# Pooling v of batch 0 and adding the halves of w_theta on VectorE and GpSimd instead of TensorE, in a hand-ordered attention and mixing kernel

## The chip, the core and the metric

The kernel runs on one core of a Trainium2 chip. A core has five engines with a queue of instructions each: TensorE (PE in the profile, its weight loads PEld), VectorE (DVE), ScalarE (ACT), GpSimd (POOL) and SyncE (SP, which here issues the DMAs). An engine takes its instructions strictly in the order in which the program put them, and they wait for each other through semaphores. SBUF is the working memory of 128 partitions. PSUM holds what TensorE writes; DVE and ACT can read it, and in this kernel GpSimd never does.

The metric is the device time of the program in microseconds (us).

## The reference

Pooled attention over 8 batches, 8 heads, 576 positions and 64 channels a head, followed by a mixing block of width 512. All of it is float32 except the weight matrices, which arrive as float64 words:

```python
k_p = k.reshape(B, H, Sp, pool, D).mean(axis=3)      # pool = 8, Sp = 72
v_p = v.reshape(B, H, Sp, pool, D).mean(axis=3)
attn = softmax(q @ k_p^T / sqrt(D));  x = attn @ v_p  # x: B, 576, 512
theta = x @ w_theta
zr, zi = x * cos(theta), x * sin(theta)
y = w_tok_r @ zr + w_tok_i @ zi                       # over the 576 positions
u = x + y
out = u + max(u @ w_ch, 0)
```

## The kernel before

Every batch passes through the same pieces, and each piece is a Python generator that issues a few instructions and yields. Their names are those of the schedule:

- `k`, `v`: the loads of k and v of a batch (0 and 1 are the two main halves, 2 the remainder of 8 pooled rows a head). `K`, `V`: the pooling over 8 neighbours; `K0`, `V0` without a number behind the dot place the pooled tiles for the matmuls (transposed keys in `kpT`, a block-diagonal `Ve` and `Vr` for the values).
- `Q`: loads of q and their transposes. `S`: scores of one tile of 128 positions (`s`), maximum (`mx`), exponential (`e_eps`, `spare`), reciprocal (`ri`), normalised weights (`en`), and for batches 0 and 1 their transposes (`pe`, `per`) on TensorE. `X`: attention output `xT` by `pv`.
- `h0` to `h3`: the four 128-row pieces of w_theta. `w`, `W`: pieces of the token weights w_tok_r and w_tok_i and their transposes `wt` into `WTh`, `WTl`. `c`: w_ch.
- `T`: theta of one tile (`pt`), sine and cosine, products into `z`, with transposes `px`. `Z`: the split of z into a high and a low half (`zh`, `zl`). `M`: mixing over positions (`py`, 27 matmuls each). `F`: the last product (`pf`, 12 matmuls each) and the store.

A float64 weight is taken apart in `to_f32`: two 32-bit words become a leading part `t` and a rest `s`, whose sum is the weight in float32. It is then split into a high part and a low part in TensorE's faster float32 format (`th`, `tl` for w_theta), so that three products stand for one in float32.

Nothing schedules the program: `SCHEDULE` is a list of some 1,900 words written out beforehand, each word advances one piece by one step, and the letter behind it (v, g or a) says which engine takes a step that could go to several. So the order of the words is the order of every queue, SP's included, and the letters spread the elementwise work over DVE, POOL and ACT.

In the kernel before, the flag `V_ON_PE = 1` makes batch 0's values be pooled on TensorE: `pool_on_pe` (L509) multiplies each of the eight neighbours by the identity and lets PSUM add them up, in tile `vpp`. From there DVE copies into `Ve` (L590) and writes `Vr` (L595). K_ON_PE does the same for k of batch 0 and is left alone. The pieces of w_theta are added on TensorE too: `channel_weights` multiplies `t` and `s` by the identity into one PSUM tile `ths` (L351, L352), from which `th` is written with a scale (L355 or L357) and `tl` as the difference (L359).

Batch 0 has a long start of its own: all weights have to be taken apart, split and transposed before its first `py`, while softmax and theta of batch 0 run. Then come seven more batches that overlap with one another.

Of the kernel before, what the change touches and what calls it, by code (L numbers as in the profile page):

```python
# [15 lines left out]
ALU = mybir.AluOpType  # L16
# [26 lines left out]
w4.0 w4.0 W2a W2 T0.1 T0.4a T0.4g T0.3 T0.2 T0.2 T0.2a Q1.2a W2 T0.2 T0.2 T0.2 W2v W2 T0.3 T0.3 v1.1 V1.1g w4.0a
T0.4 w4.0a w4.0 T0.3 T0.3 w3.0v w4.0 Q1.4 W3 T0.4 T0.4 T0.4 T0.4 Q1.4 T0.3a c0 c0 K1 T0.3 T0.3 T0.3 W3a W3 T0.4
# [85 lines left out]
F7.3.1 F7.3.1 F7.3.1 F7.3.0 F7.3.0 F7.3.0 F7.3.1  # L130
"""

EARLY, EXACT, V_ON_PE, K_ON_PE, Q_ON_PE, SUMS_ON_ACT = 2, 1, 1, 1, 2, 2


@with_exitstack
def tile_attn_moe(  # L140
    ctx: ExitStack,
    tc: tile.TileContext,
# [986 lines left out]
```

## Time and profile before

| what | us |
|---|---|
| three runs: median (lowest to highest) | 628.44 (627.2 to 629.33) |
| the profiled execution: its own time | 629.07 |
| its span, first to last instruction | 627.3 |
| 1 core, granted TensorE clock | 0.996 of full |

The profile is one execution, recorded instruction by instruction. Its page gives busy time by engine; other views of the same trace group the instructions by line and shape, follow back the chain of waits that ended last, list a stretch in order of time, or sum the busy time of each engine over chosen stretches. A busy engine is not by itself one that holds up the end: PE's matmuls are pipelined and their ends modelled, so that the busy times of neighbours overlap. Kernel lines are written L517 and so on. Behind the edited function the lines of the changed kernel have numbers lower by two, so that L443 before is L441 after.

### The profile page before, as it was taken

How to read it: one execution, taken by the hardware profiler on the slowest of the kernel's cores; microseconds unless marked ns; L12 is line 12 of the kernel's file. 1: busy time of each engine (PE TensorE's matmuls, PEld its weight loads, DVE VectorE, ACT ScalarE, POOL GpSimd, SP SyncE). 2: the span in 40 equal slices, each digit the busy share in tenths (PEclk: the TensorE clock that was granted, in tenths of full speed). 3: DMA queues.
4: the chain of work that ended last, by engine and by line, in shares of the span. 5: the costliest groups of instructions: out<-in, count | busy, mean ns of one | idle time of the engine just before them, and what ended most of it. 6: DMA issues, size and time to landing. Idle time of an engine off the chain costs nothing.

```text
span 627.3 us, 11459 instructions
## 1 busy us (share of the span) xinstructions
PE 591.2 (94%) x4120; PEld 545.7 (87%) x4120; DVE 481.5 (77%) x878; ACT 312.6 (50%) x674; POOL 350.2 (56%) x380
## 2 busy tenths in 40 slices
PE   4889979999899999899999999999999999999995
PEld 4766769988799879899899989989998999998995
DVE  5599988988897889878967898877886689456433
ACT  4769857688742556247534553237314451345000
POOL 5346545756484656565574667667675375611430
PEclk9999999999999999999999999999999999999999
DMA  9946212475465556554726356443362340511015
GB/s 295 266 135 190 67 43 77 81 124 118 91 125 99 98 100 125 100 95 82 129 58 108 63 107 120 75 85 56 52 100 51 68 65 5 79 20 30 9 20 77
DMA packets 235129, 57.85 MB, mean 92 GB/s; under 512 B 223168, under 2 KB 223680, under 8 KB 235072
## 3 DMA queue, kind: packets, MB, share of 16 engines
q1 hardware_dynamic: 233888, 56.97, 45.2%
q8 instruction: 33, 0.54, 0.4%
q10 hardware_dynamic: 1184, 0.15, 0.2%
q14 instruction: 24, 0.20, 0.1%
HBM read 37.81 MB, written 9.44 MB: 75 GB/s over the span
## 4 chain that ended last, share of the span: by engine, by line
PE 59%; DVE 14%; SPq 10%; DMA 7%; ACT 4%; issue 3%; POOL 3%; DVEq 0%; POOLq 0%; ACTq 0%
PE py L954 24%; PE pf L983 12%; PE pt L888 11%; SPq L814 8%; PE pv L861 4%; PE s L670 3%; DMA out_dram<-R 2%; PE px L898 2%; DMA eraw<-G 1%; DMA WTh_st<-in_moe_w_theta_dram 1%; SPq L1008 1%; DVE kpst L443 1%; DVE R L1002 1%; DMA kpst<-in_k_dram 1%; DVE xT L960 1%
## 5 line engine op out<-in xcount | busy, mean ns | idle before, releaser
L954 PE MATMUL py<-WTh,zh 128*128 128x256 f32 (+1 forms) x576 | 86.5, 297 | 4.4 <-DVE xT L960 2.8
L954 PE MATMUL py<-WTl,zh 128*128 128x256 f32 (+1 forms) x576 | 87.3, 296 | 0.0
L954 PE MATMUL py<-WTh,zl 128*128 128x256 f32 (+1 forms) x576 | 86.0, 294 | 1.0 <-DVE xT L960 1.0
L954 PEld LDWEIGHTS py<-WTh,zh 128*128 128x128 f32 x576 | 80.1, 189 | 5.3 <-DVE xT L960 3.0
L954 PEld LDWEIGHTS py<-WTl,zh 128*128 128x128 f32 x576 | 80.4, 190 | 0.0
L954 PEld LDWEIGHTS py<-WTh,zl 128*128 128x128 f32 x576 | 78.0, 188 | 1.6 <-DVE xT L960 1.2
L940 POOL TENSOR_TENSOR zl<-z,zh 128x640 fp32r<-128x640 f32 (+1 forms) x40 | 59.5, 1509 | 29.4 <-ACT zh L175 28.9
L967 POOL TENSOR_TENSOR ul<-xT,uh 128x320 fp32r<-128x320 f32 (+1 forms) x41 | 34.6, 849 | 43.6 <-DVE uh L177 29.1
L960 DVE TENSOR_TENSOR xT<-py,xT 128x256 f32<-128x256 f32 (+1 forms) x64 | 28.4, 445 | 35.1 <-PE py L954 35.0
L892 ACT ACTIVATE g<-pt,c_magic 128x512 f32<-128x512 f32 x38 | 26.1, 686 | 44.6 <-PE pt L888 36.2
L983 PE MATMUL pf<-uh,chh 128*128 128x256 f32 (+1 forms) x256 | 47.1, 305 | 0.3 <-DVE xT L960 0.3
L888 PE MATMUL pt<-th,xh 128*128 128x512 f32 x160 | 45.3, 405 | 1.4 <-DVE g L894 0.8
L983 PE MATMUL pf<-ul,chh 128*128 128x256 f32 (+1 forms) x256 | 44.8, 296 | 0.0
L983 PE MATMUL pf<-uh,chl 128*128 128x256 f32 (+1 forms) x256 | 44.5, 296 | 0.0
L894 DVE SCALAR_TENSOR_TENSOR g<-g,pt 128x512 f32<-128x512 f32 x38 | 25.8, 680 | 24.1 <-ACT g L892 23.8
L175 ACT CAST uh<-xT 128x320 fp32r<-128x320 f32 (+1 forms) x28 | 12.0, 434 | 63.2 <-DVE xT L960 63.1
L888 PE MATMUL pt<-th,xl 128*128 128x512 f32 x160 | 43.3, 393 | 0.0
L725 ACT ACTIVATE e_eps<-e_eps 128x576 f32<-128x576 f32 (+1 forms) x30 | 20.6, 686 | 45.4 <-DVE e_eps L721 45.3
L888 PE MATMUL pt<-tl,xh 128*128 128x512 f32 x160 | 43.1, 391 | 0.0
L865 ACT ACTIVATE xT<-pv 128x320 f32<-128x320 f32 (+1 forms) x41 | 16.8, 410 | 51.3 <-PE pv L861 45.6
L881 POOL TENSOR_TENSOR xl<-xT,xh 128x512 fp32r<-128x512 f32 x22 | 30.0, 1368 | 20.2 <-ACT xh L175 16.6
L989 DVE SCALAR_TENSOR_TENSOR oT<-pf,xT 128x256 f32<-128x256 f32 (+1 forms) x64 | 28.5, 449 | 14.2 <-PE pf L983 13.5
(252 smaller groups left out, 1491.6 us busy)
## 6 DMA issues: line engine op xcount, KB each, us to landing
out_dram<-R SPq DMA_DIRECT2D x112, 72.0 KB, 2.1
kpst<-in_k_dram SPq DMA_DIRECT2D x15, 512.0 KB, 3.9
vpst<-in_v_dram SPq DMA_DIRECT2D x28, 256.0 KB, 3.9
qsst<-in_q_dram SPq DMA_DIRECT2D x96, 72.0 KB, 2.4
eraw<-G SPq DMA_DIRECT2D x96, 60.0 KB, 2.2
eraw<-G SPq DMA_DIRECT2D x96, 40.0 KB, 2.1
WTh_st<-in_moe_w_theta_dram SPq DMA_DIRECT2D x4, 512.0 KB, 8.6
wcraw<-in_moe_w_ch_dram SPq DMA_DIRECT2D x4, 512.0 KB, 3.3
```

Source lines behind the costliest of these rows:

```text
L814: nc.sync.dma_start(blocks(Ex, jj, i), blocks(Gx, i, jj))
L861: nc.tensor.matmul(pv[:, :gn], l, r, start=i == 0, stop=i == len(terms) - 1)
L881: ENG[pick()].tensor_tensor(xl, xT[:, :, o], f32(xh), ALU.subtract)
L888: nc.tensor.matmul(pt, l[:, c, :], r[:, c, :], start=i == 0, stop=i == 11)
L892: nc.scalar.activation(g, pt, AF.Identity, bias=c_magic)
L894: nc.vector.scalar_tensor_tensor(g, g, MAGIC, pt, ALU.subtract, ALU.subtract)
L940: ENG[pick()].tensor_tensor(zl[:, r], z[:, r, o], f32(zh[:, r]), ALU.subtract)
L954: nc.tensor.matmul(py[:, :n], l[:, kk, :], r[:, kk, t], start=i == 0, stop=i == 3 * NK - 1)
L960: nc.vector.tensor_tensor(u, py[:, :n], u, ALU.add)
L967: ENG[pick()].tensor_tensor(ul[:, c, t], u, f32(uh[:, c, t]), ALU.subtract)
L983: nc.tensor.matmul(pv[:, :n], l[:, kk, o], uhl[r][:, kk, t], start=i == 0, stop=i == 11)
L989: nc.vector.scalar_tensor_tensor(oT, pv[:, :n], 0.0, xT[:, c, t], ALU.max, ALU.add)
```

## The change

Three edits. First, `V_ON_PE` becomes 0, so that `pool` takes its other branch for v of batch 0: three additions in SBUF for each of the three loads (`pool_sum`, L439, halving 512 to 64 columns), each on the engine that the schedule names. `Ve` and `Vr` then read the pooled tile in SBUF, so that their engine is free to be GpSimd too. Second, in `channel_weights` the two matmuls into PSUM are replaced by one elementwise addition of `s` to `t` in SBUF, on DVE or GpSimd, and the scale and the difference that followed read `t` in SBUF in place of the PSUM tile. Third, the whole `SCHEDULE` is replaced, for all eight batches.

```diff
 SCHEDULE = """
-k0.0 w0.0 k0.1 K0.0 K0.1 w0.0 w0.0a w0.0g w0.0 h0 h0 h0g h0a h0 h0 h0v h1 k0.2 h1 h1a h1a h1 h1 h1g Q0.0 K0.0a
...
+D w0.0 w0.0 w0.0v w0.0a h0 h0 h0a w0.0 h0a h0 h0 k0.0 K0.0 h0g h0v K0.0v h1 h1 h1v h0v h0 h1a h1 h1 k0.1 K0.1
...
-EARLY, EXACT, V_ON_PE, K_ON_PE, Q_ON_PE, SUMS_ON_ACT = 2, 1, 1, 1, 2, 2
+EARLY, EXACT, V_ON_PE, K_ON_PE, Q_ON_PE, SUMS_ON_ACT = 2, 1, 0, 1, 2, 2
...
-    def channel_weights(c, w, held_of, scale, raw_of, tmp_of, bank_of):
+    def channel_weights(c, w, held_of, scale, raw_of, tmp_of):
...
-        if bank_of is None:
+        if scale is None:
...
         hi, lo = held_of()
-        sum_ = bank([P, DM], *bank_of(c))
-        nc.tensor.matmul(sum_, ident, t, start=True, stop=False)
-        nc.tensor.matmul(sum_, identr, s, start=False, stop=True)
+        ENG[pick()].tensor_tensor(t, t, f32(s), ALU.add)
         yield
         if pick() == "a":
-            nc.scalar.activation(hi[:, c, :], sum_, AF.Copy, scale=scale)
-        else:
-            nc.vector.tensor_scalar(hi[:, c, :], sum_, scale, None, ALU.mult)
+            nc.scalar.activation(hi[:, c, :], t, AF.Copy, scale=scale)
+        else:
+            ENG[pick()].tensor_scalar(hi[:, c, :], t, scale, None, ALU.mult)
         yield
         nc.vector.scalar_tensor_tensor(
-            lo[:, c, :], sum_, scale, f32(hi[:, c, :]), ALU.mult, ALU.subtract
+            lo[:, c, :], t, scale, f32(hi[:, c, :]), ALU.mult, ALU.subtract
         )
```

What the new order does to the queues is seen at three places.

SP, the first DMAs of the program, before (raw words of w_tok_r are `wraw`, of w_theta `WTh_st`; `kpst`, `early` and `kprst` are the three loads of k):

```order
L461 DMA kpst_0_106<-in_k_dram 128x2x512
L380 DMA wraw_0_108<-in_moe_w_tok_r_dram 128x1152
L461 DMA early<-in_k_dram 128x2x512
L329 DMA WTh_st<-in_moe_w_theta_dram 128x1024 x2
L473 DMA kprst_144<-in_k_dram 64x512
L571 DMA qsst_0_153<-in_q_dram 128x8x64
```

and after:

```order
L378 DMA wraw_0_119<-in_moe_w_tok_r_dram 128x1152
L329 DMA WTh_st<-in_moe_w_theta_dram 128x1024
L459 DMA kpst_0_135<-in_k_dram 128x2x512
L329 DMA WTh_st<-in_moe_w_theta_dram 128x1024
L459 DMA early<-in_k_dram 128x2x512
L471 DMA kprst_168<-in_k_dram 64x512
L569 DMA qsst_0_189<-in_q_dram 128x8x64 x2
```

The same seven loads come first, but the weights are now in front of k, and the second load of q has moved up behind the first.

PE, from the scores of tile 2 to those of tile 4 of batch 0, before:

```order
L670 MATMUL s_2_265<-kpT,qT_152 128x144 x4
L517 MATMUL vpp_304<-early,ident 128x128 x8
L578 MATMUL pq_4_316<-ident,qst_314 128x64 x4
L760 MATMUL pe_0_324<-ident,en_0_272 128x128 x4
L670 MATMUL s_3_0_330<-kpT,qT_152 128x144 x2
L760 MATMUL pe_1_336<-ident,spare 128x128 x4
L517 MATMUL vpp_304<-early,ident 128x128 x8
L519 MATMUL vpp_304<-vprst_369,ident 64x64 x8
L662 MATMUL s_4_383<-kpT,qT_152 64x72 x8
```

and after:

```order
L668 MATMUL s_2_292<-kpT,qT_188 128x144 x4
L758 MATMUL pe_1_318<-ident,spare 128x128 x4
L758 MATMUL pe_0_331<-ident,en_0_261 128x128 x4
L766 MATMUL per_0_337<-ident,en_0_261 64x128
L668 MATMUL s_3_0_349<-kpT,qT_188 128x144 x2
L766 MATMUL per_1_360<-ident,spare 64x128
L660 MATMUL s_4_378<-kpT,qT_188 64x72 x8
```

The three poolings of v are gone between the scores; the 12 warm-up products (`warm`), which stood between the scores of tile 0 and tile 1, are now the first rows of PE.

DVE, in the same stretch, from the maximum of tile 1 on, after:

```order
L702 TENSOR_REDUCE mx_1_232<-s_1_1_227 128x4
L177 COPY qT_188<-pq_2_236 128x4x128
L441 TENSOR_TENSOR early<-early 128x2x256
L441 TENSOR_TENSOR early<-early 128x2x128
L727 RECIPROCAL ri_0_259<-sm_0_248 128x8
L730 TENSOR_TENSOR en_0_261<-e_eps,ri_0_259 128x512
L177 COPY qT_188<-pq_3_263 128x4x128
L355 TENSOR_SCALAR th<-WTh_st 128x512
L357 SCALAR_TENSOR_TENSOR tl<-WTh_st,th 128x512
L177 COPY qT_188<-pq_4_285 128x4x64
L702 TENSOR_REDUCE mx_2_298<-s_2_292 128x8
```

and before:

```order
L704 TENSOR_REDUCE mx_1_231<-s_1_1_226 128x4
L313 TENSOR_SCALAR chh_st<-wsrc_a 128x576
L729 RECIPROCAL ri_0_249<-sm_0_238 128x8
L177 COPY qT_152<-pq_2_252 128x4x128
L177 COPY qT_152<-pq_3_259 128x4x128
L704 TENSOR_REDUCE mx_2_270<-s_2_265 128x8
```

Between the same two maxima DVE now also has two sums of v, a normalisation that GpSimd did before, and `th` and `tl` of a piece of w_theta.

More of the change, by code (lines that the diff above doesn't have):

```diff
@@ new lines @@
+T3.2 T3.2 S4.2 T3.3g T3.3g T3.3 T3.3 T3.4g F2.2.0 T3.4v T3.3 T3.3 E4.0a E4.0g E4.0g E4.0g F2.2.1 F2.2.1 T3.3
+F2.2.0 F2.2.1 K5 S4.3g S4.3g T3.3a T3.4 T3.3 T3.3 T3.3 S4.4 T3.4 T3.4 T3.4 T3.4 Q5.1 Q5.1 T3.4 T3.4 F2.3.1
+F2.3.1 V4g F2.3.0 F2.3.0 X4.0.0 X4.0.0v K5a K5 K5a S5.0 S4.3 Z3.0g X4.0.1 Z3.0g X4.0.1a Z3.1a Z3.1v M3.0.0
+M3.0.0 M3.0.0g S4.4 S4.4 S4.4v S4.4g S5.0 X4.0.2 X4.0.2a M3.0.1 M3.0.1 S4.4 X4.0.3 X4.0.3a T4.0v Q6.0 M3.0.0v
+T4.0g M3.0.1a M3.0.1g S5.0 S5.0 S5.0v v5.1 V5.1g M3.1.1 M3.1.1 M3.1.1a E4.2 S5.1 S5.0v S5.1 S5.1 M3.1.0 S5.1
@@ L1054, in tile_attn_moe @@
                 ),
-                lambda c: ("mm", f"ths{c}", 2),
             ),
```

194 lines of the change are left out of this document (94 added, 100 removed).

## The prediction

> **What bounds the kernel now.** First the page, for the span and the busy shares, then the busy time of each engine by stage (columns: stretch, its length, busy us of PE, PEld, DVE, ACT, POOL, each with its count, then clock, DMA share, GB/s). The stages follow events of the trace: 18.60 is where the first scores of batch 0 start, 34.90 the scores of tile 4, 53.50 the first theta, 91.10 the end of the weights' preparation.
>
> ```profile
> span 627.3 us, 11459 instructions
> PE 591.2 (94%) x4120; PEld 545.7 (87%) x4120; DVE 481.5 (77%) x878; ACT 312.6 (50%) x674; POOL 350.2 (56%) x380
> 5.60:18.60 13.00, 9.43 (x56) 7.24 (x55) 5.22 (x9) 6.68 (x14) 6.36 (x4) 0.87 1.12 309
> 18.60:34.90 16.30, 14.71 (x134) 13.93 (x135) 11.51 (x23) 12.42 (x68) 6.45 (x7) 1.00 0.78 219
> 34.90:41.00 6.10, 4.45 (x35) 2.57 (x31) 5.82 (x15) 4.34 (x16) 3.96 (x6) 1.00 0.15 28
> 41.00:53.50 12.50, 12.34 (x61) 7.31 (x62) 11.66 (x21) 10.40 (x31) 6.06 (x8) 1.00 0.76 238
> 53.50:70.00 16.50, 16.20 (x93) 12.54 (x91) 16.26 (x25) 14.85 (x24) 8.83 (x7) 1.00 0.68 181
> 70.00:91.10 21.10, 15.73 (x107) 13.09 (x106) 19.01 (x31) 16.27 (x30) 12.10 (x10) 1.00 0.09 33
> 95.10:124.00 28.90, 28.20 (x215) 27.65 (x215) 25.49 (x50) 21.09 (x80) 18.42 (x21) 1.00 0.34 85
> 124.00:627.30 503.30, 484.93 (x3406) 456.31 (x3404) 378.51 (x693) 223.92 (x414) 283.62 (x308) 1.00 0.44 79
> ```
>
> The page alone says TensorE, 94%. By stage it is two kernels. From 95.1 on PE is busy 28.20 of 28.90 and 484.93 of 503.30. Before that PE shares the bound with VectorE: from 34.9 to 91.1 DVE is busy 5.82 + 11.66 + 16.26 + 19.01 = 52.75 of 56.2 us. Only from 5.6 to 34.9 has DVE room: 29.3 less 16.73, so 12.6 us. Everything that the change takes from PE stands before 46 us, so the start decides, and there the chain of waits (start, length, what) is the view to read:
>
> ```profile
> 16.64 1.65 PE ths L351 x2
> 18.29 0.23 PE ths L352
> 19.88 2.68 PE warm L257 x24
> 27.92 1.78 PE vpp L517 x16
> 32.10 1.79 PE vpp L517 x16
> 33.89 1.01 PE vpp L519 x15
> 35.00 0.42 DVE Ve L177
> 35.42 0.12 DVE Ve L177
> 36.28 0.49 DVE mx L704
> 43.63 1.94 DVE WTl_st L324
> 45.61 0.50 PE ths L352
> 91.12 4.01 PE py L954 x27
> ```
>
> From 16.6 to 35 the chain runs mainly over PE, with all three poolings of v and one sum of w_theta in it. Behind that it is DVE's, until `py` begins.
>
> **The change, part by part.** Durations are means of the groups by line and shape (busy us, mean ns behind the bar):
>
> ```profile
> L517 PE MATMUL vpp<-early,ident 128*128 128x128 f32 x32 | 3.9, 275 | 0.0
> L351 PE MATMUL ths<-WTh_st,ident 128*128 128x512 f32 x8 | 5.0, 716 | 0.0
> L352 PE MATMUL ths<-WTl_st,identr 128*128 128x512 f32 x4 | 3.2, 812 | 0.2 <-DVE WTl_st L324 0.2
> L443 DVE TENSOR_TENSOR vpst<-vpst 128x512 f32<-128x512 f32 x3 | 2.4, 808 | 0.0
> L443 DVE TENSOR_TENSOR vpst<-vpst 128x256 f32<-128x256 f32 x3 | 1.3, 426 | 0.1
> L443 DVE TENSOR_TENSOR vprst<-vprst 64x256 f32<-64x256 f32 x2 | 0.9, 462 | 0.0
> L448 DVE TENSOR_TENSOR vp<-vpst 128x128 f32<-128x128 f32 x3 | 0.9, 292 | 0.1
> L339 DVE TENSOR_TENSOR wcts<-wcts 128x512 f32<-128x512 f32 x4 | 3.2, 809 | 0.1
> L359 DVE SCALAR_TENSOR_TENSOR tl<-ths,th 128x512 fp32r<-128x512 f32 x4 | 2.6, 678 | 0.0
> L732 DVE TENSOR_TENSOR en<-e_eps,ri 128x512 f32<-128x512 f32 x16 | 12.8, 799 | 0.6
> L177 DVE COPY eh<-pe 128x512 f32<-128x512 f32 x2 | 1.4, 686 | 0.2 <-PE pe L760 0.2
> ```
>
> *Removed from PE.* The busy sums are 3.9 for the main halves of v, about 1.0 for the remainder (1.01 in the chain), 5.0 + 3.2 for the sums of w_theta: 13.1 us. What counts is the part on the chain up to 35 us: 1.65 + 0.23 for `ths`, 1.78 + 1.79 + 1.01 for `vpp`, 6.46 together. The 12 `warm` products move to the first rows of PE, where it has nothing else yet: another 2.68 off this stretch. The two copies into `Ve` go to GpSimd, 0.54. Sum **9.7 us**. The three later sums of w_theta cost the chain 0.50 where they stood, since DVE was late there.
>
> *Added to DVE* ahead of the maximum of tile 4, counted in the order of the two programs: for v two sums of 128x512, one of 128x256, one of 128x128 and three of 64 rows (taken at 0.46, 0.46 and 0.29, a bound from above): 1.62 + 0.43 + 0.29 + 1.21 = 3.5. For w_theta two sums at 0.81 and two more `tl` at 0.68: 3.0. Two normalisations that GpSimd did: 1.6. Given up: two copies `eh` 1.4, one copy of q 0.7, `Ve` 0.5 to 0.8. The word conversions, three more L306 and two `th`, stand against four conversions given up; I take these as even. Net about **+5.4 us**, and from there to `py` the two orders, counted in the same way, give DVE as much work as each other to within 1 us (four more conversions, one sum of w_theta and one pooling of k of batch 1 stand against copies of `eh`, `er` and `xT` that go to ACT). A sum in SBUF has no row before in just this place; its ends are 0.69 (a DVE sum with GpSimd at rest, below 0.75 for 128x576 in the next rows) and the 1.93 of the same rows; I take 0.81, the group nearest to it.
>
> *What is late next.* Between 5.6 and 34.9 DVE has 12.6 us free and takes 5.4 of them. ACT has 19.10 of 29.3 busy there and gets about 2.7 more, and its exponentials, one tile after another, begin only with the first scores: 12.42 of 16.30 busy, so with 2.7 more it has 15.1 to do behind them. That leaves 16.30 − 15.1 = 1.2 us to win behind the first scores. Ahead of them, the scores themselves can come earlier by the 1.88 of `ths`, unless the loads, now with the weights in front of k, eat it. Together **−3 us** (from 0, if ACT and DVE hand it on with one wait more, to −9.7 if neither holds anything).
>
> *The stretch from 35 to 91 us.* DVE is busy 94% of it; the work is the same to within 1 us either way, so the 3 us are kept and nothing is added: 0 ± 2.
>
> *From `py` on.* PE has the same instructions as before. Up to the first `pf` DVE gets about 2 us more, in a stage with 28.90 − 25.49 = 3.4 us free: 0. The later order differs in hundreds of places, but PE's idle time there is 503.30 − 484.93 = 18.4 us, several of them at the very end, where the last products and stores are alike. I take 0, between −3 and +3.
>
> Sum −3 us. The profiled execution took 629.07 with a span of 627.3, which is 0.6 above the median of 628.44; −3 on the median is **625.5**, and 624.3 would be the span.
>
> **The rivals.** *Full gain.* If PE alone bound the start, 9.7 to 13.1 us would go: 616 to 619. For it speaks the chain from 16.6 to 35; against it DVE's 52.75 of 56.2 behind it.
>
> *Nothing comes through.* If ACT's row of exponentials holds tile 4 where it was, the freed PE time becomes idle time: 628.
>
> *Slower, by GpSimd and DVE in each other's way.* The timeline (start, length) has this:
>
> ```profile
> 31.33 0.75 DVE L324 TENSOR_TENSOR wsrc_b<-wsrc_b,wpow 128x576 fp32r<-128x576 f32 x1
> 37.40 1.05 POOL L732 TENSOR_TENSOR en<-e_eps,ri 128x512 f32<-128x512 f32 x1 [0.73 <-DVE ri L729]
> 37.43 1.33 DVE L306 TENSOR_SCALAR wsrc_b<-wraw 128x576 fp32r<-128x576 uint32 x1
> 43.60 1.40 POOL L324 TENSOR_TENSOR wsrc_b<-wsrc_b,eraw 128x576 fp32r<-128x576 f32 x1 [3.16 <-DVE eraw L317]
> 43.63 1.93 DVE L324 TENSOR_TENSOR WTl_st<-WTl_st,eraw 128x512 fp32r<-128x512 f32 x1
> ```
>
> The same DVE operation took 0.75 with GpSimd at rest and 1.93, on a smaller tile, when it started 0.03 behind a GpSimd instruction; it ended 0.56 after that one's end. The change puts 14 instructions with both operands in SBUF on DVE before `py` (seven sums of v, three of w_theta, four `tl` whose first operand was in PSUM) and five more L306: 19 that can be caught. At GpSimd's share of 6.06 in 12.50 nine would be, for up to 1.93 − 0.75 = 1.2 us each: 11 us if each starts right behind GpSimd's instruction, 5 if it starts in the middle of it. It decides from three full waits on, which use up the 3 us; at 6 to 7 us it gives 632. Against it: in the stage from 18.6 to 34.9, where most of the 19 go, GpSimd is busy 6.45 of 16.30 only, and the new order takes work from it ahead of tile 4's maximum (two L306, two products L324 and two normalisations, against one sum of v, one of w_theta and the copies into `Ve`).
>
> The Trainium skill, page "SBUF — State Buffer", section "Who interferes with whom", speaks against the change here: a DVE instruction with two inputs in SBUF contends with a GpSimd one that reads SBUF, and the later one blocks for the whole of it, while one with a single SBUF input outside the two-port modes does not. By that rule the old `tl` from PSUM was safe and the new one is not; the pair at 43.6 agrees with it.
>
> **How the numbers follow.** Forecast 622 to 627, most likely 625.5: 0.48. Full gain: 0.09. Nothing comes through, 627 to 629.5: 0.21. Slower, 629.5 to 634: 0.22. The range that holds 8 in 10 goes from 618, half-way into the full gain, to 632.5, past the middle of the slower case. Faster by over 0.3%, about what a measurement of this kernel can tell from no change, means under 626.5: nine tenths of the forecast's 0.48 and all of the full gain's, 0.52. Slower means over 630.3: all but a tenth of the last case, 0.20. Within: 0.28.
>
> **What would show it.** The maximum of tile 4 (36.28 in the chain) some 3 us earlier, and `py` (91.12 for its second group) by as much; DVE over 90% busy from the first scores to `py`; PE with more idle time before `py` than now. Wrong would be: `py` earlier by 8 us or more (PE was the bound); tile 4 earlier but `py` not (the waits behind GpSimd, seen as DVE sums of over 1.2 us); or a change that arises behind 124 us, where I put nothing.

## The result, and the profile after

The changed kernel is slower: a median of 633.78 us (631.22 to 636.87, 20 runs) against 629.32 (624.72 to 633.8, 20 runs) of the kernel before on the same chip, a ratio of **1.0066 (95% interval 1.0044 to 1.0089)**. The forecast of 625.5 missed, and the median lies above the range of 618 to 632.5, on the side of the third rival. The profiled execution after took 633.44 with a span of 631.7; its mean granted clock was 0.974, before 0.996. All ratios here and below leave out one execution, the only slow one on record: 1266.97 us in e11.

First the page after, then its busy time by stages of before (stretch, length, busy us of PE, PEld, DVE, ACT, POOL with counts, clock, DMA share, GB/s):

```profile
span 631.7 us, 11355 instructions
PE 591.5 (94%) x4060; PEld 548.7 (87%) x4060; DVE 479.2 (76%) x883; ACT 304.9 (48%) x655; POOL 355.9 (56%) x407
```

```profile
5.60:18.60 13.00, 9.17 (x58) 7.99 (x57) 6.63 (x12) 6.01 (x14) 1.27 (x1) 0.74 1.11 276
18.60:34.90 16.30, 9.07 (x57) 8.34 (x58) 14.03 (x28) 12.56 (x63) 6.64 (x7) 0.79 1.08 295
...
41.00:53.50 12.50, 8.61 (x43) 6.24 (x44) 12.01 (x22) 8.10 (x24) 3.88 (x5) 0.73 0.42 147
```

PE was relieved as meant: from 18.6 to 34.9 it has 57 matmuls and 9.07 us instead of 134 and 14.71. DVE took the work, 14.03 instead of 11.51. New is the clock, third column from the right: 0.73 to 0.79 in three of the stages up to 53.5, where it was 0.87 in the first and 1.00 in the others.

Four events place the loss. The timeline of DVE (start, length), before:

```profile
19.92 0.76 DVE L704 TENSOR_REDUCE mx<-s 128x8 f32<-128x576 f32 x1 [3.86 <-PE s L670]
36.21 0.74 DVE L704 TENSOR_REDUCE mx<-s 64x8 f32<-64x576 f32 x1
59.24 0.68 DVE L894 SCALAR_TENSOR_TENSOR g<-g,pt 128x512 f32<-128x512 f32 x1
92.02 0.42 DVE L960 TENSOR_TENSOR xT<-py,xT 128x256 f32<-128x256 f32 x1
```

and after:

```profile
20.09 0.76 DVE L702 TENSOR_REDUCE mx<-s 128x8 f32<-128x576 f32 x1
37.62 0.74 DVE L702 TENSOR_REDUCE mx<-s 64x8 f32<-64x576 f32 x1
60.98 0.69 DVE L892 SCALAR_TENSOR_TENSOR g<-g,pt 128x512 f32<-128x512 f32 x1 [1.25 <-ACT g L890]
96.52 0.41 DVE L958 TENSOR_TENSOR xT<-py,xT 128x256 f32<-128x256 f32 x1
```

The rows are the first maximum, tile 4's maximum, the first product of theta and the first eviction of `py`. They shifted by +0.2, +1.4, +1.7 and **+4.5**; the span grew by 4.4. So the profiled loss is there by the first `py`, and most of it arises between theta and `py`. Behind `py` a gain and a loss cancel, as e3 will show.

The chain of waits after, around tile 4's maximum (start, length, what):

```profile
33.39 1.85 PE s L668 x8
35.27 0.46 DVE mx L702
...
35.92 0.13 DVE vpr L446
...
36.16 0.34 DVE Vr L593
36.50 0.82 DVE WTl_st L306
37.62 0.74 DVE mx L702
```

The poolings of v on PE are gone from the chain. In their place tile 4's maximum stands in DVE's queue, behind `vpr` and `Vr`, which DVE now works on, and a word conversion.

### The profile page after: what moved, and what is told of

Same layout as the page of the kernel before. It is cut to its first block, busy times and chain, and to the rows that moved or that the text cites. A ratio compares the mean times of both kernels' runs of the same rounds, so it can differ in the third digit from the quotient of the medians.

```text
span 631.7 us, 11355 instructions
## 1 busy us (share of the span) xinstructions
PE 591.5 (94%) x4060; PEld 548.7 (87%) x4060; DVE 479.2 (76%) x883; ACT 304.9 (48%) x655; POOL 355.9 (56%) x407
## 4 chain that ended last, share of the span: by engine, by line
PE 76%; DVE 12%; DMA 5%; ACT 3%; issue 2%; POOL 1%; SPq 1%; DVEq 0%; ACTq 0%; POOLq 0%
PE py L952 34%; PE pt L886 14%; PE pf L981 12%; PE pv L859 5%; PE s L668 4%; PE px L896 2%; DMA out_dram<-R 1%; DMA kpst<-in_k_dram 1%; DMA vprst<-in_v_dram 1%; PE kpp L515 1%; DMA wraw<-in_moe_w_tok_i_dram 1%; DVE mx L702 1%; DVE en L737 1%; DVE g L919 1%; SPq L1006 1%
## 5 line engine op out<-in xcount | busy, mean ns | idle before, releaser
L952 PE MATMUL py<-WTh,zh 128*128 128x256 f32 (+1 forms) x576 | 88.0, 300 | 1.3 <-ACT zh L175 0.6
L965 POOL TENSOR_TENSOR ul<-xT,uh 128x256 fp32r<-128x256 f32 (+1 forms) x39 | 34.2, 890 | 44.3 <-DVE uh L177 25.7
L879 POOL TENSOR_TENSOR xl<-xT,xh 128x512 fp32r<-128x512 f32 x28 | 38.3, 1371 | 13.1 <-ACT xh L175 7.0
L890 ACT ACTIVATE g<-pt,c_magic 128x512 f32<-128x512 f32 x38 | 26.1, 686 | 37.1 <-PE pt L886 32.5
L981 PEld LDWEIGHTS pf<-uh,chh 128*128 128x128 f32 x256 | 37.8, 191 | 3.7 <-DVE oT L987 3.3
L668 PE MATMUL s<-kpT,qT 128*128 128x144 f32 x256 | 38.7, 294 | 2.0 <-ACT qT L175 1.3
```

Source lines behind the costliest of these rows:

```text
L668: nc.tensor.matmul(scs[c // 2][:n, 2 * SP * (c % 2) : 2 * SP * (c % 2 + 1)], qT[:, c, t0 : t0 + n], kpT[:, c, :], start=True, stop=True,)
L879: ENG[pick()].tensor_tensor(xl, xT[:, :, o], f32(xh), ALU.subtract)
L890: nc.scalar.activation(g, pt, AF.Identity, bias=c_magic)
L952: nc.tensor.matmul(py[:, :n], l[:, kk, :], r[:, kk, t], start=i == 0, stop=i == 3 * NK - 1)
L965: ENG[pick()].tensor_tensor(ul[:, c, t], u, f32(uh[:, c, t]), ALU.subtract)
L981: nc.tensor.matmul(pv[:, :n], l[:, kk, o], uhl[r][:, kk, t], start=i == 0, stop=i == 11)
```

## The experiments

Several kernels below share their start word for word, so their profiles repeat it. The first maximum scatters in such repetitions (19.92, 19.28 and 20.39 with before's start, 20.09, 19.95, 18.52 and 18.85 with after's), but the distance from it to tile 4's maximum does so by 0.1 us at most. To `py` it scatters by 0.2 with before's start and by 1.1 with after's (76.4 to 77.5 in after, e4 and e13). The table therefore gives distances, from one profiled execution each: from the first maximum to tile 4's and to the first `py` eviction, and from the first output row `oT<-pf` to the last. The ratios are to executions of before on the same chip as the run; the runs were on five chips. Line numbers of these kernels differ by a few from the changed kernel's.

| run | ratio to before (95%) | first max | to tile 4 | to `py` | `oT` first to last |
|---|---|---|---|---|---|
| before | 1 | 19.9 | 16.3 | 72.1 | 494.7 |
| after | 1.0066 (1.0044–1.0089) | 20.1 | 17.5 | 76.4 | 494.7 |
| e1_fill | 1.0074 (1.0041–1.0108) | 18.6 | 16.6 | 78.0 | 497.3 |
| e2_v_on_pe | 1.0021 (0.9991–1.0050) | 18.6 | 20.2 | 80.6 | 491.2 |
| e3_old_start | **0.9937** (0.9905–0.9968) | 19.3 | 16.3 | 72.1 | 489.6 |
| e4_new_start | 1.0040 (1.0017–1.0064) | 19.9 | 17.6 | 77.5 | 490.7 |
| e5_sums_only | 1.0116 (1.0081–1.0152) | 18.7 | 17.8 | 81.3 | 494.0 |
| e6_v_only | 1.0050 (1.0022–1.0078) | 17.7 | 20.8 | 79.7 | 490.8 |
| e7_sums_on_pe | 1.0104 (1.0063–1.0144) | 18.4 | 19.3 | 82.8 | 491.3 |
| e8_old_loads | 1.0134 (1.0097–1.0171) | 25.1 | 17.4 | 78.2 | 494.1 |
| e9_fill_old_second | 1.0027 (1.0001–1.0054) | 18.7 | 16.6 | 76.5 | 495.8 |
| e10_old_second | 1.0063 (1.0029–1.0097) | 18.5 | 17.6 | 74.5 | 495.9 |
| e11_new_second | 0.9989 (0.9962–1.0017) | 20.4 | 16.3 | 76.2 | 488.5 |
| e12_no_sums | 1.0040 (1.0009–1.0071) | 18.6 | 17.2 | 75.4 | 495.4 |
| e13_unlock_late | 1.0085 (1.0055–1.0115) | 18.5 | 17.6 | 77.1 | 495.9 |
| e14_dve_twice | 1.0178 (1.0140–1.0217) | 20.4 | 19.5 | 82.5 | 496.9 |
| e15_less_gpsimd | 1.0088 (1.0057–1.0120) | 18.9 | 17.6 | 76.1 | 494.9 |
| e16_unlock_before | 0.9969 (0.9945–0.9993) | 20.4 | 16.3 | 72.3 | 491.9 |
| e17_before_twice | 1.0053 (1.0026–1.0080) | 19.7 | 16.5 | 74.6 | 496.7 |
| e18_pe_less | 0.9950 (0.9911–0.9989) | 18.6 | 15.3 | 73.1 | 490.4 |

### Is it the clock? e1

PE's gaps in the new start are followed by a halved clock. e1 is the changed kernel with unused products, 12 more in the warm-up and 57 in the gaps:

```diff
-        for _ in range(12):
+        for _ in range(24):
...
+    def fill(n, tag="th"):
+        fills.append(n)
+        p = bank([P, 512], tag, f"fill{len(fills)}")
+        for _ in range(n):
+            nc.tensor.matmul(p[:, 0:P], ident, ident, start=True, stop=True)
```

> The changed kernel with 58 more unused products of the identity with itself on PE, in banks that nobody reads, at the places where PE waited in its start: 12 more warm-ups, 10 ahead of the transposes of q's last tile (PE idle 2.47 us there), 15 ahead of the first pe of tile 1 (3.84), 4 and 11 ahead of the first two pv (1.16 and 2.77), 6 ahead of the second piece of W0 (1.51), 11 ahead of W4 (2.77). DVE, ACT, GpSimd and all DMAs are as they were. Theory A (PE idles, its granted clock falls to about half, and kpp, pe, s, pv, wt and pt on the chain run slowly): granted clock at or near 1.00 from 10 us on, the first pt back from 4.42 to about 2.8 us, the first py eviction from 96.5 to 92 to 93.5, time 629 to 631. Theory B (DVE and GpSimd in each other's way) and theory C (the new order makes PE wait for DVE whatever PE's clock is): the clock rises, but the first py eviction stays within 1 us of 96.5 and the time at 633 to 635.

Busy time in three stretches, after and then e1:

```profile
8.00:12.00 4.00, 3.37 (x16) 3.40 (x16) 1.81 (x3) 1.96 (x3) 1.27 (x1) 0.50 1.21 266
28.00:32.00 4.00, 0.76 (x4) 0.79 (x5) 3.93 (x10) 1.87 (x12) 0.09 (x1) 0.52 1.04 410
44.00:48.00 4.00, 4.00 (x18) 2.81 (x17) 3.75 (x7) 1.86 (x5) 1.37 (x1) 0.50 0.72 258
```

```profile
8.00:12.00 4.00, 2.70 (x22) 2.32 (x21) 1.99 (x5) 1.96 (x3) 1.27 (x1) 1.00 1.25 271
28.00:32.00 4.00, 3.39 (x29) 3.01 (x27) 3.93 (x10) 3.10 (x19) 1.60 (x2) 1.00 1.03 394
44.00:48.00 4.00, 3.26 (x17) 2.21 (x16) 3.96 (x8) 3.10 (x6) 2.44 (x3) 0.77 0.16 65
```

The fills hold most of the clock, and tile 4's maximum comes 16.6 us behind the first one instead of 17.5 to 17.6 (e9, with the same fills there, has 16.6 too). So 1.0 of the 1.3 us by which that distance grew is the clock's. By `py` it is gone, 78.0 for 76.4 to 77.5, and the ratio is after's. The halved clock is real, but with these fills, which also give PE 57 products more, holding it up did not win the loss back.

### Which part? e2, e5, e6, e7

e2 puts v of batch 0 back on PE in the changed kernel; its PSUM tile moves to the bank of the pooled k.

```diff
-EARLY, EXACT, V_ON_PE, K_ON_PE, Q_ON_PE, SUMS_ON_ACT = 2, 1, 0, 1, 2, 2
+EARLY, EXACT, V_ON_PE, K_ON_PE, Q_ON_PE, SUMS_ON_ACT = 2, 1, 1, 1, 2, 2
```

> The changed kernel in its own order, but v of batch 0 pooled by PE again (its bank is the one of the pooled k); the sums of w_theta stay on DVE. DVE loses some 3.5 us of sums ahead of tile 4's maximum, PE gets 4.6 us back between 20 and 36 us. Theory A: PE's idle gaps ahead of pe are partly filled and the clock there rises; first py eviction 94 to 95, time 631 to 632. Theory B: half of the DVE sums that GpSimd can catch are gone; 631 to 632 as well, but with the clock as low as before. Theory C (order alone): 633 to 634.

e7 puts the sums of w_theta back on PE:

```diff
-        ENG[pick()].tensor_tensor(t, t, f32(s), ALU.add)
+        sum_ = bank([P, DM], "mm", f"ths{c}", 2)
+        nc.tensor.matmul(sum_, ident, t, start=True, stop=False)
+        nc.tensor.matmul(sum_, identr, s, start=False, stop=True)
```

> The changed kernel in its own order, with the sums of w_theta back on PE; v stays with DVE and GpSimd. DVE loses 2.8 us, 2 of them ahead of the first theta; PE gets 8.2 us back, in the stretches where it was idle and its clock low. Theory D: first theta from 61.0 to 59, first py eviction 94 to 95, ratio to before 1.001 to 1.004. Theory A: the clock rises too, and gives as much again: 92 to 93, ratio 0.998 to 1.001. Theory C (the order alone): 96 to 97, ratio 1.005 to 1.009.

e6 is the kernel before with v alone moved (the letters give the steps their engines):

```diff
-EARLY, EXACT, V_ON_PE, K_ON_PE, Q_ON_PE, SUMS_ON_ACT = 2, 1, 1, 1, 2, 2
+EARLY, EXACT, V_ON_PE, K_ON_PE, Q_ON_PE, SUMS_ON_ACT = 2, 1, 0, 1, 2, 2
-V0.0 ... V0.1 ... V0.2 V0v V0
+V0.0v V0.0g V0.0v ... V0.1v V0.1v V0.1g ... V0.2v V0.2v V0.2v V0v V0v
```

> The kernel before in its own order, with the other part alone: v of batch 0 pooled by DVE (one of the sums by GpSimd), the sums of w_theta on PE as before. DVE gets 3.5 us of sums, some 2 of them ahead of the first theta's use of v, PE loses 4.6. Theory D: first py eviction 94 to 96, ratio 1.003 to 1.007. Theory A: as far as the granted clock falls below 1.00 between 30 and 40 us, 1 to 2 us, ratio 1.001 to 1.003. The prediction's reasoning: a gain of up to 4 us.

e5 is the kernel before with the sums alone moved; the high half of the first piece of w_theta holds other numbers there, with the same amount of work.

```diff
-        sum_ = bank([P, DM], *bank_of(c))
-        nc.tensor.matmul(sum_, ident, t, start=True, stop=False)
-        nc.tensor.matmul(sum_, identr, s, start=False, stop=True)
+        ENG[pick()].tensor_tensor(t, t, f32(s), ALU.add)
```

> The kernel before in its own order, with one part of the change alone: the four sums of w_theta on DVE, none on PE. DVE gets 4 sums of 0.69 us, 2.8 in all, PE loses 8.2. Theory D (VectorE's own work bounds the start: from the first scores to the first theta it was idle 1.2 us in the kernel before and not at all in the changed one, so whatever it is given comes out at py): first py eviction from 92.0 to 93.5 to 95, time ratio to before 1.002 to 1.005. Theory A (PE's clock is what costs): PE keeps the poolings of v, clock stays at 1.00, no loss: ratio 0.997 to 1.001. The prediction's own reasoning (PE is on the chain up to 35 us) would give a gain of 1 to 2 us.

All four took longer to `py` than before and after, 79.7 to 82.8. Each puts one part into an order drawn up for the other case, and PE waits at the head of its queue: 3.50 us at `ths` in e7, 3.18 at `pe` in e6, 2.79 at `pe` in e2. In e5 the clock was 0.50 from 38.5 to 62.4 us, with PE busy for 22.20 of these 23.90, so that there the low clock is a likely part of the loss. So they don't give the prices of the parts. They show that a part and the order drawn up for it belong together.

### Which stretch of the order? e3, e4, e11, e10, e9

These kernels are spliced out of the two orders. e3 and e4 cut where `Z0.0` begins, close to the first `py`: e3 has the start of before (v and sums on PE) and then after's order, e4 the reverse.

```diff
 W3 T0.4 T0.4 K1a c0g w4.0g
-c0 c0 c0 c0v W4 Z0.0a Z0.0v M0.0.0
+Q1.4a k2.2 K1 K1v Z0.0a c0 c0 c0 c0g W4
```

> The kernel before up to the end of its preparation of weights (first take of z), then the order of the changed kernel for everything behind it. If the loss arises in the start (A, B or C alike), this is 626 to 630, first py eviction at 92. If the later order is what costs, 632 to 635.

```diff
 T0.4 T0.4 W3 w4.0g T0.4 T0.4
-Z0.0a c0 c0 c0 c0g W4 W4a
+c0 c0 c0 c0v W4 Z0.0a Z0.0v M0.0.0
```

> The changed kernel up to the same place, then the order of the kernel before. If the loss arises in the start, 632 to 635, first py eviction at 96.5, and all later ones about 4.5 us behind those of the kernel before. If the later order is what costs, 628 to 630.

**e3 is faster than both kernels**: 626.24 us, 0.9937 of before. After, with its new start, is 1.0066 / 0.9937 = 1.013 of e3. So the later order is worth 0.6% by itself, and the new start, with whatever follows from it later, costs 1.3%.

e11, e10 and e9 have one cut more, at the first theta. e11 has before's order up to there, then after's to the end; e10 has after's, then before's up to `Z0.0`, then after's; e9 is e10 with e1's fills up to theta.

```diff
 w2.0 w2.1 w2.1a w2.1a w2.1 T0.0
-T0.0 w2.0 T0.0 w3.0 w1.1g W1 W1v
+w3.0 Q1.2 w1.1v w2.1 T0.0 T0.0 W1 w3.0
```

> The mirror of it: the kernel before (v and w_theta on PE) up to its first theta, then the order of the changed kernel. Theory E: first theta 58.6 to 59.2 as before, then 35.5 us or more instead of 32.8, first py eviction 94 to 96, ratio 0.997 to 1.003 (the run with the whole old start and the same later order had 0.9937). If the order behind the first theta does not matter: 91 to 92, ratio 0.991 to 0.996.

```diff
 w2.1 w2.1 w2.0 w2.0a w2.0a w2.0
-T0.0 T0.0 W1 w3.0 X0.2.2 W1a W1
+T0.1v X0.2.3 X0.2.3v X0.2.0v T0.0 w2.0 T0.0 W1 W1v W1
```

> The same three pieces without the unused products. Theory E: first theta 60 to 61, first py eviction 93 to 94, ratio to before 0.996 to 1.001. If the order behind the first theta does not matter: 96 to 97, ratio 1.004 to 1.008.

```diff
+            fill(10)
...
+            fill(15)
```

> Three pieces: the changed kernel up to the first theta, with the unused products of the run before it in PE's gaps up to there (47 of them: without those ahead of W4); then the order of the kernel before up to the first take of z; then the order of the changed kernel. Theory E (two causes: PE's low clock and DVE's added work up to the first theta, and behind it the order, in which GpSimd holds DVE up and both wait for PE): first theta 57.8, from there to the first py eviction 32.8 us as in the kernel before, so 90.6, the earliest of all; ratio to before 0.990 to 0.996. If the longer way from theta to py follows from the earlier pieces and not from that order: 93 to 96, ratio 0.998 to 1.006.

From the first maximum to `py` this makes a table of two by two:

| us to `py` | old order from theta on | new order from theta on |
|---|---|---|
| old start (v, sums on PE) | 72.1, 72.1, 72.3 (before, e3, e16) | 76.2 (e11) |
| new start (v, sums on DVE and GpSimd) | 74.5 (e10) | 76.4, 77.5, 77.0 (after, e4, e13) |

The new order of the second stretch costs 4.1 us by itself, with every product of v and w_theta still on PE. The new start alone costs 2.4, and on top of the new second stretch 0.2 to 1.3. The cuts at theta also carry some work across it: theta comes 38.0 us behind the first maximum in e11, 41.7 in e10, and 39.3 to 40.9 in the uncut orders. So the table counts from the first maximum.

At the end the picture is less simple. e10 and e9 were expected at 0.996 to 1.001 and 0.990 to 0.996, and came out at 1.0063 and 1.0027. e10 reaches `py` 1.9 to 3.0 us sooner than the kernels with the new second stretch, and still has after's ratio: the way from the first maximum to its first `oT` is only 0.5 us shorter than after's (109.7 for 110.2), and that from its first `oT` to the last 1.2 longer. The second stretch explains the loss at `py`, not the whole of the loss at the end.

What holds the second stretch? Its busy time (columns as above) from theta to `py` in before and e3 (old order), then in after and e11 (new order):

```profile
59.24:92.02 32.78, 27.11 (x170) 22.24 (x170) 30.43 (x50) 26.03 (x46) 15.81 (x14) 1.00 0.24 70
```

```profile
58.61:91.34 32.73, 27.88 (x174) 22.78 (x173) 31.19 (x52) 27.16 (x49) 16.70 (x16) 1.00 0.28 72
```

```profile
60.98:96.52 35.54, 32.06 (x190) 25.86 (x190) 31.82 (x53) 27.84 (x47) 24.21 (x23) 0.95 0.29 82
```

```profile
58.43:96.66 38.23, 31.21 (x183) 24.94 (x183) 35.34 (x54) 26.24 (x43) 25.25 (x23) 0.96 0.35 91
```

To tell DVE's own work from being held up, I took for each operation and shape the 20th-percentile duration over the twenty traces as its undisturbed length, and summed over the stretch that and what the instructions took above it (neighbouring instructions overlap a little, so the two sums together can exceed the stretch):

| theta to `py` | us | undisturbed | above it |
|---|---|---|---|
| before, e3, e10 (old order) | 32.7 to 32.8 | 29.8, 30.3, 29.9 | 3.1, 3.5, 2.4 |
| after, e4, e11 (new order) | 35.5 to 38.2 | 29.8, 29.6, 29.8 | 4.6, 7.0, 8.0 |

The same DVE work takes longer, beside 21 to 23 GpSimd instructions of 23 to 25 us instead of 14 to 16 of 16 to 17. One pair of rows shows it, the same operation on `wsrc_a` in before and then in e11, the latter with the GpSimd instruction that ran when it began:

```profile
63.22 0.75 DVE L315 SCALAR_TENSOR_TENSOR wsrc_a<-wsrc_a,chh_st 128x576 int32<-128x576 int32 x1
```

```profile
62.87 1.63 POOL L319 TENSOR_TENSOR wsrc_b<-wsrc_b,eraw 128x576 fp32r<-128x576 f32 x1
63.29 1.83 DVE L310 SCALAR_TENSOR_TENSOR wsrc_a<-wsrc_a,chh_st 128x576 int32<-128x576 int32 x1
```

That is the third rival's mechanism, in another place than it named. How much of the longer way it accounts for differs: the time above grew by 4.9 of 5.4 us in e11 and by 3.9 of 5.1 in e4, but in the changed kernel itself by 1.5 of 2.8. There the new order also leaves PE more to do behind theta, 190 matmuls instead of 170, with 12 `pv` instead of 4. In the chain of waits of e11 24.3 of the 38.2 us are DVE's, in e4 23.8 of 37.9, in before 18.2 of 32.8; in after 25.1 of 35.5 are PE's and 3.6 DVE's, and up to 79.7 us it stays on PE:

```profile
64.52 2.79 PE pv L859 x8
67.31 0.59 PE px L896 x4
67.89 2.76 PE pt L886 x12
```

So waits of DVE and more work for PE are both there, and no run separates them. The clock of 0.95 and 0.96 does not by itself lengthen the stretch: e6 and e18 have the old order with 0.95, and take 32.8 us.

To test the link to GpSimd directly, e15 gives two GpSimd instructions of that stretch to DVE:

```diff
-W2 W2a T0.3g T0.2g T0.2 T0.3g w4.0
+W2 W2a T0.3g T0.2v T0.2 T0.3v w4.0
```

> The changed kernel with two letters changed: xl of tiles 2 and 3 of batch 0 (1.3 to 1.8 us each on GpSimd, between first theta and first py) are done by DVE in 0.68 each. DVE gets 1.4 us more and GpSimd loses some 3. Theory B: DVE's time above the undisturbed durations in that stretch falls from 4.6 to 7.9 us by 2 or more, so the stretch from first theta to first py eviction goes from 35.5 to 38.8 to 34.5 to 36.5 although DVE has more to do; ratio 1.003 to 1.007. If GpSimd does not hold it up: the stretch gets longer by 1 to 1.4 us, ratio 1.007 to 1.010.

Theta to `py` took 36.5 us, between after's 35.5 and e4's 37.9; DVE's own work there rose to 31.2, the time above it was 5.0. Inconclusive: what GpSimd gave up, DVE got. So the link from GpSimd's longer time to DVE's is shown as going together (above 2.4 to 3.5 in before and all eight kernels with the old order there, 4.6 to 8.0 in after and all ten with the new one), not by taking it away.

### How much room has DVE? e17, e14, e12, e18

e17 runs nine word conversions twice in the kernel before, some 4 us of DVE work; e14 does the same in the kernel after.

```diff
+        twice.append(1)
+        if len(twice) <= 9:
+            nc.vector.tensor_scalar(pi, ti, -0x800000, None, ALU.bitwise_and)
```

> The kernel before with the same nine masking instructions L317 of its start done twice on DVE, as in the run of the changed kernel; PE keeps all its work. DVE gets 4 us more. Theory D (DVE's own work bounded the start already before the change, so the 5.4 us that the change gives to DVE had to come out): first theta from 59 to 62 to 65, first py eviction from 92 to 95 to 99, ratio to before 1.005 to 1.011. If DVE had the free time there on which the forecast counted (12.6 us between 5.6 and 34.9): first py within 1 us of 92, ratio 0.998 to 1.003.

> The changed kernel with nine DVE instructions of its start done twice (the masking L317, which gives the same numbers again, 0.43 to 0.46 us each; two of them ahead of the first scores). DVE gets 4 us more, 3 of them between the first scores and the first theta. Theory D (DVE's own work bounds that stretch): first theta from some 60 to 61 to 62.5 to 64, first py eviction 99 to 101, ratio to before 1.009 to 1.013. If DVE has room there: 96 to 97.5 and 1.005 to 1.008.

The way to `py` became 2.5 us longer in e17 (74.6 for 72.1), and 5.0 to 6.1 in e14 (82.5 for 76.4 to 77.5). Here are before, e17 and after from the first maximum to theta:

```profile
19.92:59.24 39.32, 35.91 (x246) 26.84 (x245) 34.66 (x65) 31.22 (x117) 21.59 (x24) 1.00 0.69 199
```

```profile
19.73:61.56 41.83, 37.32 (x252) 27.64 (x250) 38.07 (x72) 32.05 (x117) 22.43 (x25) 1.00 0.67 192
```

```profile
20.09:60.98 40.89, 28.05 (x149) 20.69 (x147) 37.17 (x72) 29.31 (x120) 14.75 (x17) 0.79 0.66 187
```

DVE has 39.32 − 34.66 = 4.7 us free in before, of which e17's 3.4 us of more busy time could use 0.9; in that order the rest are waits in its queue that don't move. After has 2.5 us more busy time than before on DVE, and 7.9 us less on PE. Of the 2.5 it fits 0.9 into DVE's free time; e4, e13 and e15, with the same words up to there, fit in 2.1 (37.1 busy of 39.6 to 39.7).

e12 drops from the kernel after the four sums of `s` (w_theta is then its leading part alone):

```diff
-        ENG[pick()].tensor_tensor(t, t, f32(s), ALU.add)
```

> The changed kernel without the four DVE sums of w_theta (4 x 0.69 us): th and tl are made of the high words alone, so the low words of w_theta are missing in the result; nothing else is changed, nothing is put on PE. Theory D (DVE's own work bounds the stretch to the first theta): first theta from 61.0 to 59 to 60, and py and the end 1 to 2.8 us earlier: ratio 1.002 to 1.005. If DVE's added work is hidden: unchanged, 1.005 to 1.009.

To `py` 75.4, 1.0 to 2.2 us less than with them, and 1.0040.

e18 is the counterpart: PE relieved in the kernel before, with nothing given to DVE. Of the neighbours of v only the first of eight is multiplied, and of the two summands of w_theta only the rest, so v of batch 0 and w_theta hold other numbers. That is 9.0 of the 13.1 us.

```diff
-        nc.tensor.matmul(sum_, ident, t, start=True, stop=False)
-        nc.tensor.matmul(sum_, identr, s, start=False, stop=True)
+        nc.tensor.matmul(sum_, identr, s, start=True, stop=True)
...
+        n = 1 if name == "vp" else POOL
```

> The kernel before with PE's work taken away and given to nobody: of the pooling of v of batch 0 only the first of eight rows is summed, of each sum of w_theta only the low words (v of batch 0 and w_theta are wrong in the result); PE loses 4.0 and 5.0 of the 13.1 us that the change takes from it, DVE, ACT, GpSimd and the order are as before. This is the gain of the change without its price. The forecast's steps: tile 4's maximum (36.2) 2 to 4 us earlier, and py as much: ratio 0.992 to 0.997. Theory D: DVE bounds the stretch, so tile 4's maximum may come earlier but first theta and first py eviction by less than 1.5 us: ratio 0.997 to 1.001.

Its busy time from 36 to 48 us, and before's:

```profile
36.00:48.00 12.00, 12.00 (x44) 8.12 (x43) 9.48 (x17) 7.38 (x26) 6.37 (x8) 0.52 0.75 225
```

```profile
36.00:48.00 12.00, 10.72 (x54) 6.46 (x54) 11.64 (x24) 8.52 (x30) 5.40 (x8) 1.00 0.68 210
```

Tile 4's maximum came 1.0 us sooner behind the first (15.3 for 16.3), `py` 1.0 later (73.1 for 72.1). In between PE was busy for all of 12 us at a clock of 0.52, and DVE for 9.48 instead of 11.64. I read this as the clock taking back what was taken from PE; no run holds the clock up in e18. (Its ratio of 0.9950 comes from later stages, where this run is 4 us shorter from the first `oT` to the last.)

### Why does a gain behind `py` vanish? e13, e16

The `oT<-pf` rows, matched one by one, give how far a kernel lags behind e3, which has the same later order (head: the time in e3):

| lag behind e3, us | 125 | 441 | 489 | 503 | 508 | 613 |
|---|---|---|---|---|---|---|
| after | 5.1 | 4.8 | 6.3 | 6.7 | 10.7 | 10.3 |
| e8 | 11.9 | 11.0 | 12.5 | 12.8 | 16.9 | 16.5 |
| e14 | 11.5 | 13.2 | 14.7 | 15.5 | 18.6 | 18.8 |
| e11 | 5.5 | 5.1 | 5.1 | 4.9 | 5.2 | 4.5 |
| e2 | 7.6 | 9.5 | 9.5 | 9.5 | 9.5 | 9.2 |

In the first three the lag grows by 1.5 us between 441 and 489 and by 3 to 4 between 503 and 508; in e11 and e2, with the same words there, it does not. The timeline at that place, after:

```profile
510.58 1.04 POOL L628 TENSOR_TENSOR Vr<-vrx,mask 96x512 fp32r<-96x512 f32 x1
510.86 3.40 DVE L919 TENSOR_SCALAR g<-g 64x512 int32<-64x512 int32 x1
511.58 2.39 POOL L833 TENSOR_TENSOR eraw<-eraw,eh 128x1024 fp32r<-128x1024 f32 x1
516.18 1.14 PE L981 MATMUL pf<-uh,chh 128*128 128x256 f32 x4 [2.57 <-DVE oT L987]
```

and e3:

```profile
504.33 0.42 DVE L916 TENSOR_SCALAR g<-g 64x512 int32<-64x512 int32 x1
504.42 0.89 POOL L622 TENSOR_TENSOR vrx<-vpr,vrh 32x64 f32<-32x64 f32 x2
506.76 0.67 PE L978 MATMUL pf<-uh,chh 128*128 128x256 f32 x4
```

The same small DVE instruction on `g` took 0.42 where it started 0.09 ahead of a GpSimd instruction, and 3.40 where it started 0.28 behind one. It ended at 514.26, 0.29 after the second of two GpSimd instructions back to back, and PE stood for 2.57 us. The Trainium skill, page "SBUF — State Buffer", section "Who interferes with whom", says that whoever issues first holds the shared port for the whole instruction; the pair agrees, except that the wait did not end with the first instruction.

e13 gives that subtraction, `eraw`, to DVE in the kernel after:

```diff
-F5.3.0 V7g V7g E7.0g Z6.0g
+F5.3.0 V7g V7g E7.0v Z6.0g
```

> The changed kernel with one letter changed: the last subtraction of batch 7's turn (eraw L833, 2.39 us on GpSimd at 511.58) is done by DVE. In the changed kernel a DVE instruction g L919 started at 510.86 between two GpSimd instructions and took 3.40 us instead of 0.42, ending with GpSimd's; PE then waited 2.57 for pf and ran at a clock of 0.83. Theory B (DVE held up while GpSimd works): the stall goes, the end comes 2.5 to 4 us earlier, ratio to before 1.000 to 1.003, first py eviction unchanged at 96 to 97.5. If that stall is chance or harmless: 1.005 to 1.008.

```profile
512.63 1.15 DVE L914 TENSOR_SCALAR g<-g 64x512 int32<-64x512 int32 x1
515.71 0.73 PE L976 MATMUL pf<-uh,chh 128*128 128x256 f32 x4 [0.32 <-DVE oT L982]
519.25 0.39 PE L854 MATMUL pv<-eraw,Vh 128*128 128x256 f32 x1 [1.62 <-DVE eraw L828]
```

The long wait went (1.15 for 3.40, PE's gap 0.32 for 2.57), and a new one of 1.62 came behind the moved instruction. From 503 to 548 the lag behind e3 grows by 1.9 us instead of 3.8, but the ratio shows no gain, 1.0085.

The kernel before had such a place at 259 us, a pooling of k on DVE that begins beside a row of GpSimd instructions:

```profile
259.00 5.88 DVE L443 TENSOR_TENSOR kpst<-kpst 128x512 f32<-128x512 f32 x2 [1.74 <-DMA kpst<-in_k_dram]
258.54 2.56 POOL L881 TENSOR_TENSOR xl<-xT,xh 128x512 fp32r<-128x512 f32 x2
261.07 2.80 POOL L940 TENSOR_TENSOR zl<-z,zh 128x640 fp32r<-128x640 f32 x2
265.66 1.10 PE L954 MATMUL py<-WTh,zh 128*128 128x256 f32 x7 [2.77 <-DVE xT L960]
```

e16 moves that pooling to GpSimd, behind the splits of `z`:

```diff
-T3.0g T3.1a k5.0 K5.0v T3.1g
+T3.0g T3.1a k5.0 T3.1g
...
-Z2.2a Z2.2g M2.1.1g
+Z2.2a Z2.2g M2.1.1g K5.0g
```

> The kernel before with one step given to GpSimd and moved behind its next instructions: the last pooling of k of batch 5 by DVE (L443, at 259.00) took 5.43 us for the first of two sums of 128x512 and 128x256 that take 1.2 together where GpSimd rests, while four GpSimd instructions ran one after the other, and PE waited 2.77 us for DVE's copy behind it. Theory B: PE's stall at 263 goes, the end comes 2 to 4 us earlier, ratio to before 0.994 to 0.997. If the loss is made up later anyway, or GpSimd's later work stalls PE in its place: 0.998 to 1.002.

Its output rows lag 2.0 us behind before's at 235 us and lead them by 0.5 at 284: 2.5 us were gained there. The ratio is 0.9969. Another DVE instruction was caught in its turn, a copy into `uh` of 5.07 us, but nobody waited for that one.

### The order of the first loads: e8

e8 is the kernel after with the first loads in before's order:

```diff
-D w0.0 w0.0 w0.0v w0.0a h0 h0 h0a
+D k0.0 w0.0 k0.1 h0 h1 k0.2 w0.0 w0.0v w0.0a h0 h0a
```

> The changed kernel with only the first six loads in the order of the kernel before: k0.0, w0.0, k0.1, h0, h1, k0.2, where it had w0.0, h0, k0.0, h1, k0.1, k0.2. The pooling of k begins at 4.4 instead of 8.6 us, so the first scores come 2 to 3 us earlier (first maximum from 20.1 to 17 to 18), where DVE had idle time. Theory D: from the first maximum on DVE is full, so first theta and py follow by the same 2 to 3 us: first py eviction 93.5 to 95, ratio 1.001 to 1.004. If the later part of the start is bound by PE's order (theory C), first theta moves and py does not: ratio 1.005 to 1.008.

The first maximum came at 25.1, and the ratio was 1.0134. PE waited 5.39 us for the copies of the pooled keys, which stand in DVE's queue behind work on `h1`, whose load now came later. The place of the loads was part of the new order, not a cost of it.

## Why the prediction was wrong

**Step 1, what leaves PE: right in the counts, worth little.** The prediction took the 9.7 us on PE's chain as what could be won at most, and let 3 come through. e18, with PE relieved and nothing given to DVE, won 1.0 at tile 4's maximum and lost it by `py`. The step had no term for the granted clock, which was 0.52 over 12 us in e18, behind a gap of 1.93 us on PE.

**Step 2, what is late next: −3 forecast, nothing measured.** Of the −3, −1.2 were to come between the first scores and tile 4's maximum, with ACT as the limit and 2.7 us more of work for it. ACT got no more: 6.01 + 12.56 = 18.57 us from 5.6 to 34.9, for 19.10 before. That distance grew by 1.3, in four executions: 1.0 through the clock (e1, e9), the rest, as I read it, on DVE, in whose queue the maximum stands in the chain after. The failing sentence is "DVE has 12.6 us free and takes 5.4 of them": the 12.6 were counted from 5.6 on, and most of them, 13.00 − 5.22 = 7.8, lie ahead of 18.6, before the scores are there. Behind the first maximum DVE had 4.7 us free, and the new order uses 0.9 to 2.1 of them: that room took up added work, and made nothing earlier. The other −1.88, earlier scores, can't be told from the scatter of the first maximum. Theta comes 39.3 us behind the first maximum in before, e3 and e16, and 39.6, 39.6, 39.7 and 40.9 in e13, e15, e4 and after.

**Step 3, from 35 to 91 us, 0 ± 2: the step that decided the result.** The sentence that failed is "the work is the same to within 1 us either way, so the 3 us are kept and nothing is added". Its first half was right for DVE to 1.2 us (undisturbed, from tile 4's maximum to `py`, 49.1 us before and 50.3 after); that equal work takes equal time was not: from theta to `py` 35.5 to 38.2 us instead of 32.7 to 32.8, and e11 has it without any of the moved work. The prediction compared what the orders give DVE, and not what they put beside it on GpSimd, nor what they leave to PE behind theta. That the new order there is what costs is shown; how its loss divides between DVE's waits and PE's greater work in the changed kernel stays open.

**Step 4, from `py` on, 0 ± 3: right in sum, for another reason.** The new later order gains: from the first `oT` to the last e3 takes 489.6 and e11 488.5, before 494.7. After gains it too and loses it again, between 441 and 508, and ends at 494.7. That the two cancel is luck.

**The rivals.** "Slower" (632) had the sign, and a mechanism that the rows show, but put it on the 19 moved instructions from 18.6 to 53.5. From the first maximum to theta, DVE's time above the undisturbed was 5.2 us before and 5.0 after; it grew behind theta, and at 511 on a row on `g`, which no part of the change touches. "Full gain" falls with e18. Of the signs named as wrong the third came: a change behind 124 us, in e3.

**What stays open.** Why the step at 508 appears in some kernels and not in others with the same words there: it is absent in e2, e3 and e11, which pool v on PE, and present in after, e1, e7, e8, e9, e10, e12, e14 and e15, which don't. No run shows how that reaches across 400 us. Which of GpSimd's instructions behind theta costs most, e15 did not settle. And why e10, with the old second stretch, is no faster at the end than after.

## What to carry to other kernels

Compare two orders not only by the work that they give the busiest engine, but by what stands beside it on the engine that can hold it up: the stretch with equal DVE work took 8 to 17% longer here. Free time of an engine counts only between the event that releases the added work and the one that needs it; doubling a cheap instruction (e17) measures that room before a change is built. And a new order is judged in pieces, by splicing: here its later part gains 0.6% with the old start, while the whole loses 0.7%.

## What the runs showed of the hardware

**A caught DVE instruction can wait for a row of GpSimd instructions, not only for one.** In the kernel after, one on 64x512 took 3.40 us, until 0.29 behind the second of two. The one on `wsrc_a` in e11 waited for one alone: it ended at 65.12, 0.62 behind the first GpSimd instruction, while the next ran from 64.47 to 66.28. In before, a pooling that began at 259.00 beside four in a row had its two halves end only at 264.88.

**Gaps of under 4 us were followed by a halved clock.** In the kernel after, the timeline of PE has these:

```profile
8.63 3.75 PE L515 MATMUL kpp<-kpst,ident 128*128 128x128 f32 x16 [2.95 <-DMA kpst<-in_k_dram]
31.24 1.09 PE L758 MATMUL pe<-ident,spare 128*128 128x128 f32 x4 [3.84 <-DVE spare L737]
43.39 1.22 PE L859 MATMUL pv<-eh,Ve 128*128 128x256 f32 x2 [2.77 <-DVE xT L865]
```

The windows from 8, 28 and 44 have 0.50, 0.52 and 0.50. The same gap of 2.77 in before, up to 265.66, left the clock at 1.00 from 260 to 270. The Trainium skill, page "TensorE: Matmul & The Clock Gate", section "What's actually happening", has the clock halved after an idle window of about 3.4 us; gaps of 2.95 and 2.77 come in front of a halved clock here, and one of 2.77 does not, so the length of a single gap does not decide.

**A kernel's executions spread with the clock.** e3 took 622.3 us at a mean clock of 0.995 and 628.7 at 0.987, the kernel after 631.2 at 0.980 and 636.9 at 0.969. Which of the two makes the other isn't shown. One profile's span can so be off by some microseconds; the ratios rest on the medians.
